# A banded attention and a softplus MLP on one core: a new start order, score bursts and a new written order

## The chip, the cores and the metric

The kernel runs on one core of a Trainium2 chip. The metric is the device time of one execution in microseconds (us), as the median of several runs. The engines are PE (TensorE, matrix products), DVE (VectorE), ACT (ScalarE), POOL (GpSimd) and SP, which here only issues DMAs. PEld is PE's loading of weights, which overlaps its products.

## The reference

Attention with four batches, eight heads, 768 rows and a head dimension of 64. A row sees eight global keys and the 96 keys up to itself; a bias grows with the distance, and the slope depends on the head. The attention's output, 3072 tokens of 512 values, goes through two products with a softplus between them.

```python
scores = scale * np.matmul(q, k.transpose(0, 1, 3, 2))
is_global = pos[None, :] < int(n_global)            # 8
is_local = (rel >= 0) & (rel < int(n_local))        # 96
dist = np.where(is_global & ~is_local, float(n_local), np.abs(rel))
scores = scores - slopes[:, None, None] * dist      # per head
a = softmax of scores where (is_global | is_local)
x = (a @ v), rows of 8 heads side by side           # 3072 x 512
h = x @ w_in                                        # 512 x 2048
g = np.maximum(h, 0.0) + np.log1p(np.exp(-np.abs(h)))
return g @ w_out                                    # 2048 x 512
```

## The kernel before

The work is cut into 24 blocks of 128 query rows with all eight heads, and into twelve units of two neighbouring blocks of a batch, 256 rows. Blocks, units and tiles are counted from zero here. Every step is a named operation with an engine, the buffers that it reads and writes, and a function that emits its instructions. One long written table, `ORDER`, lists all names with the letter of their engine (P for PE, V for DVE, A for ACT, G for POOL, S for SP). The operations are emitted in that order, so the table is each engine's queue, and an engine works its queue strictly in order; a semaphore wait is added where an operation reads or overwrites what another engine made.

The names that matter here, with the lines of the kernel before:

- `ldq`, `ldk`, `ldv`: loads of a unit, 512 KB of each (L584, L598, L608); the first units' q and k come in halves of 256 KB. `win` and `wout` are the eight tiles of each weight, 512 KB apiece (L639). SP issues them all but the first q (ACT). They land in 14 slots called `raw`, and a slot is used again when its cast has been made.
- `castq`, `castk`, `castv`, `cin`, `cout`: casts to bf16 (L658, L674, L686, L706, L643).
- `trq`, `trk`: transposes of q and k. For the first three units PE makes them into PSUM (L790 for unit 0, in two halves; L810 after) and `cpq`, `cpk` copy them out (L793, L817); later units use DMA transposes that SP issues (L837, L830).
- `sc n`: the scores of block n on PE (L950; L897 for block 0), against the block's own keys and, for all but the first block of a batch, against those of the block before, whose first rows have been replaced by the batch's global keys. `gk` and `gv` make these copies of the global rows of k (L852, L855) and v (L868). A block's scores lie in two parts (`n.0`, `n.1`), each in one of two PSUM tiles `s_ps0` and `s_ps1`.
- `z n`: the bias added by DVE (L976); for blocks 0 and 1 PE puts the bias in before the scores instead (`sb`, L887 and L931). `ex n`: the exponential on ACT (L983). `pv n`: P·V on PE (L1002). `nm n`: a reciprocal and a product on DVE that normalise (L1013, L1014).
- `xt n`, `xc n`: the transpose of a block's x, on PE for the first six blocks (L1033, L1038), then by a DMA transpose (L1045).
- `a g.p`: for the 256 tokens of unit g the products with tile p of w_in, eight on PE (L1060), into one of two PSUM tiles `h_ps`; `e` (L1075) and `ln` (L1086) are the two ACT steps of the softplus.
- `b`: the products with w_out. Groups 0 and 1 use plain ones (L1107); later groups use a scheme with seven instead of eight products of half size (L521), for which `ws` adds up parts of w_out once (L416) and `ka` parts of the activations per group (L451), on DVE or POOL; `oe` adds the results up.
- `oc`, `st`: copies and stores of the output.
- `fill`: a 128x512 product on a constant tile `blank` into `x_ps` (L1235). Nothing uses its result.

Two things about the first unit and the bursts are set by small tables. The two halves of the first transposes of q and of k go through one and the same PSUM tile, so the second half can be made when the first has been copied out. `WHOLE` names the blocks whose two score parts are one operation of sixteen products; the others make one part, wait until its tile can be written again, and make the second. In the kernel before blocks 1, 3 and 5 are not in it.

```python
WHOLE = (0, 2, 4, 6, 7, 8, 9, 10, ..., 23)
FIRST_LOADS = "k0 q0 v0 q1 k1 v1 i1 i3 i0 i2 i4 i5 i7 i6 k2 q2 o0 ...".split()
for parts in () if n in LONE else ((0, 1),) if n in WHOLE else ((0,), (1,)):
    scores(n, parts, rank + 0.1 * parts[0])
```

## Time and profile before

| what | value |
|---|---|
| median of 3 runs | 210.56 us (210.1 to 210.59) |
| span of the profiled execution | 208.3 us |
| difference, around the span | 2.26 us |
| PE busy | 201.5 us, 97% |
| ACT busy | 169.0 us, 81% |
| DVE busy | 159.8 us, 77% |
| POOL busy | 112.8 us, 54% |
| mean granted PE clock | 0.997 |

The span runs from the first to the last instruction of the profiled execution; the time of a run is a little longer. Busy shares are means over the span. Whether an engine sets the time is read from stretches of it: PE's busy time in a stretch beside the stretch's length, and what released PE after a gap. In a row of the timeline the first number is the start, the second the duration, and brackets hold the idle time before and its releaser. In rows of groups the numbers after the bar are the busy time in us and the mean of one in ns; the row of a source line has minimum, median and maximum in ns.

### The profile page before, as it was taken

What the parts mean: (1) busy time and instruction counts of PE and PEld (TensorE: products, weight loads), DVE (VectorE), ACT (ScalarE), POOL (GpSimd) and SP (SyncE); (2) the same over time, 40 slices, a digit from 0 to 9 for tenths busy, and PEclk for the clock granted to TensorE, in tenths of its full rate; (3) what the DMA queues carried; (4) which work ended last, traced back from release to release, by engine and by line L of the source; (5) the groups of instructions that cost most, each with busy time, mean ns of one, the idle gap of its engine ahead of it and who ended that gap; (6) DMA issues with size and microseconds to landing.
All of it is one profiled execution on the core that took longest, in us unless ns stands there. A gap on an engine that the chain in (4) does not pass through costs nothing.

```text
span 208.3 us, 5515 instructions
## 1 busy us (share of the span) xinstructions
PE 201.5 (97%) x2211; PEld 164.8 (79%) x2211; DVE 159.8 (77%) x296; ACT 169.0 (81%) x240; POOL 112.8 (54%) x127
## 2 busy tenths in 40 slices
PE   7789999999999999999999999999999999999993
PEld 2455887756678889888888898888888889888882
DVE  5589899899888798786989995928897684434383
ACT  4698899998999987998879989679879895897300
POOL 4356262708686367742867699655707506623540
PEclk9999999999999999999999999999999999999998
DMA  5999999999998999679999979573742204200205
GB/s 175 364 361 388 387 358 361 332 245 249 201 271 214 257 210 312 172 188 296 195 212 259 191 200 221 145 152 102 106 73 62 92 5 142 63 0 0 104 22 181
DMA packets 70650, 40.99 MB, mean 197 GB/s; under 512 B 30433, under 2 KB 62689, under 8 KB 70625
## 3 DMA queue, kind: packets, MB, share of 16 engines
q1 hardware_dynamic: 69936, 39.99, 77.2%
q10 hardware_dynamic: 688, 0.66, 1.0%
q8 instruction: 17, 0.28, 0.5%
q14 instruction: 9, 0.07, 0.1%
HBM read 27.26 MB, written 6.29 MB: 161 GB/s over the span
## 4 chain that ended last, share of the span: by engine, by line
PE 85%; DMA 8%; DVE 2%; POOL 2%; issue 1%; ACTq 0%; ACT 0%; POOLq 0%; DVEq 0%
PE h_ps L1060 38%; PE o_ps L521 25%; PE s_ps L950 5%; PE x_ps L1002 4%; PE s_ps L1107 3%; DMA raw<-in_q_dram 3%; DMA kT<-kb 3%; DMA XT<-xs 2%; PE x_ps L1235 2%; PE x_ps L521 2%; PE s_ps L521 1%; PE s_ps L810 1%; POOL vb L706 1%; PE o_ps L1107 1%; PE o_ps L1002 1%
## 5 line engine op out<-in xcount | busy, mean ns | idle before, releaser
L1060 PE MATMUL h_ps<-XT,w_in_bf 128*128 128x256 bf16 x768 | 94.4, 273 | 0.1
L1060 PEld LDWEIGHTS <-w_in_bf 128*128 128x128 bf16 x768 | 73.2, 98 | 11.0 <-DMA XT<-xs 0.3
L1075 ACT ACTIVATE e<-h_ps 128x512 f32<-128x512 f32 x96 | 60.1, 637 | 17.6 <-PE h_ps L1060 16.6
L1086 ACT ACTIVATE g<-e 128x1024 bf16<-128x1024 f32 x48 | 49.8, 1053 | 0.6
L976 DVE TENSOR_TENSOR z<-s_ps,biasA 128x1024 f32<-128x1024 f32 x38 | 45.9, 1218 | 3.5 <-PE s_ps L950 3.1
L983 ACT ACTIVATE pb<-z 128x1024 bf16<-128x1024 f32 (+1 forms) x44 | 43.4, 993 | 1.3 <-DVE z L976 0.6
L451 POOL TENSOR_TENSOR g<-g 128x1024 bf16<-128x1024 bf16 x11 | 23.9, 2171 | 23.7 <-DVE raw L451 23.5
L521 PEld LDWEIGHTS <-g 128*128 128x128 bf16 x320 | 30.9, 98 | 3.6
L451 POOL TENSOR_TENSOR raw<-g 128x1024 bf16<-128x1024 bf16 x9 | 19.6, 2177 | 15.0 <-ACT g L1086 13.5
L868 POOL COPY vb<-vb 4x512 bf16<-4x512 bf16 x22 | 14.9, 675 | 20.9 <-PE x_ps L1002 16.2
L706 POOL CAST vb<-raw 64x512 bf16<-64x512 f32 x32 | 21.6, 678 | 6.0 <-DMA raw<-in_v_dram 4.7
L521 PEld LDWEIGHTS <-raw 128*128 128x128 bf16 x240 | 22.6, 98 | 2.8
L521 PE MATMUL o_ps<-raw,raw 128*128 128x256 bf16 x192 | 24.3, 273 | 0.0
L451 DVE TENSOR_TENSOR raw<-g 128x1024 bf16<-128x1024 bf16 x21 | 17.2, 829 | 6.5 <-ACT g L1086 4.1
L521 PE MATMUL o_ps<-raw,g 128*128 128x256 bf16 x160 | 19.6, 273 | 0.0
L1002 PEld LDWEIGHTS <-pb 128*128 128x128 bf16 x352 | 16.4, 98 | 3.6 <-ACT pb L983 0.6
L1014 DVE TENSOR_TENSOR xs<-x_ps,rcp 128x256 bf16<-128x256 f32 x40 | 17.0, 424 | 1.4
L1002 PE MATMUL x_ps<-vb,pb 128*128 128x65 bf16 x304 | 15.8, 193 | 0.0
L521 PE MATMUL o_ps<-w_out_bf,g 128*128 128x256 bf16 x128 | 15.8, 273 | 0.0
L1235 PE MATMUL x_ps<-blank 128*128 128x512 bf16 x35 | 11.7, 454 | 1.2 <-DVE blank L1159 1.2
L1013 DVE RECIPROCAL rcp<-x_ps 128x4 f32<-128x4 f32 x40 | 7.1, 178 | 7.4 <-PE x_ps L1002 6.8
L674 POOL CAST qb<-raw 128x1024 bf16<-128x1024 f32 (+1 forms) x9 | 9.3, 1032 | 5.9 <-DMA raw<-in_q_dram 5.6
(123 smaller groups left out, 216.3 us busy)
## 6 DMA issues: line engine op xcount, KB each, us to landing
raw<-in_v_dram SPq DMA_DIRECT2D x12, 512.0 KB, 5.7
out_dram<-osb SPq DMA_DIRECT2D x22, 256.0 KB, 2.5
raw<-in_q_dram SPq DMA_DIRECT2D x9, 512.0 KB, 4.9
raw<-in_k_dram SPq DMA_DIRECT2D x9, 512.0 KB, 5.5
raw<-in_moe_w_in_dram SPq DMA_DIRECT2D x8, 512.0 KB, 9.3
raw<-in_moe_w_out_dram SPq DMA_DIRECT2D x8, 512.0 KB, 9.1
raw<-in_k_dram SPq DMA_DIRECT2D x6, 256.0 KB, 5.9
raw<-in_q_dram SPq DMA_DIRECT2D x4, 256.0 KB, 7.0
```

Source lines behind the costliest of these rows:

```text
L451: (nc.vector if eng == "DVE" else nc.gpsimd).tensor_tensor(dst, a[0], b[0], ALU.subtract)
L521: nc.tensor.matmul(psum(j), lhs[:, f // 2, f % 2, :], w(f), start=(f == 0 and not (chain and j in "267")), stop=(f == 7), skip_group_check ...
L706: copy_on[eng](dst, src)
L868: copy_on[eng](vb_of(prev)[sl, :, 0:D], vb_of(first)[sl, :, 0:D])
L976: nc.vector.tensor_tensor(z, src, bias, ALU.add)
L983: nc.scalar.activation(pb[:, 0:nr, :].rearrange("p (y a) b -> p y (a b)", y=2), src, AF.Exp, scale=1.0 / root_d)
L1002: nc.tensor.matmul(xv[:, h, :], pb[:, 4 * (h % 2) + 2 * part + h // 2 if lone else u_all * (2 * (h % 2) + h // 2) + u, :], vb_of(prev if u ...
L1014: nc.vector.tensor_tensor(xs[:, 4 * part : 4 * part + 4, :], xv[:, :, 0:D], rcp[:][:, :, None].to_broadcast([P, 4, D]), ALU.mult,)
L1060: last = nc.tensor.matmul(hv[:, j, :], w_in_bf[:, m, fb * P : fb * P + P], XT[g % NXG][:, m, :], start=(m == 0), stop=(m == NM - 1),)
L1075: nc.scalar.activation(e[:, p % 2, :, :].rearrange("p j (b t r) -> p (j b) r t", b=2, r=2), hb[:].rearrange("p (a r t) -> p a r t", a=4, r=2),
L1086: nc.scalar.activation(gt[:, 2 * p - 2 : 2 * p + 2, :].rearrange("p a t -> p (a t)"), e[:].rearrange("p a j t -> p (a j t)"), AF.Ln, bias=1.0,
L1235: nc.tensor.matmul(x_ps[:], blank[:, 0:P], blank[:])
```

## The change

First, the table `ORDER` is written anew up to the middle of the kernel; from there on it differs in single places. Second, the list of first loads is put in another order, and with it the queue of SP. Third, the halves of unit 0's transposes get a PSUM tile each: q's use `s_ps0` and `o_ps`, k's `s_ps1` and `x_ps`. Fourth, blocks 1, 3 and 5 join `WHOLE`. Fifth, 28 fillers instead of 35: eleven at the start of the program and 17 after unit 0's casts and transposes have been declared; ten of them stand ahead of the first transposes in PE's queue, and the rest between later operations. Sixth, the copies of global rows no longer carry a dependency on the exponentials of the block before. Seventh, the two slots for the sums of w_out are set aside when the sums are made, not when the first tile of w_out is loaded. Line numbers move by one to four.

```diff
 ORDER = """
-ident:G ldv0:S ldq0.0:A blank:V fill0:P ldk0.0:S iota:G table:A ldq0.1:A fill1:P ldk0.1:S fill2:P dl1a:V dl0a:V
+iota:G ldk1.1:S ldq0.0:A blank:V fill0:P ldk0.0:S table:A ldq0.1:A ident:G dl0a:V fill1:P dl1a:V dl0b:V fill2:P
...
-FIRST_LOADS = "k0 q0 v0 q1 k1 v1 i1 i3 i0 i2 i4 i5 i7 i6 k2 q2 o0 o1 v2 o2 o3 o4 o5 o6 o7".split()
+FIRST_LOADS = "k0 q0 v0 q1 k1 v1 i0 i1 i2 i3 k2 q2 i4 i5 o0 o1 i6 i7 o2 o3 v2 o4 o5 o6 o7".split()
...
-FILLERS = 35
+FILLERS = 11, 28
...
+SPLIT_KEYS = {"q": (("s", 0, 0), ("o",)), "k": (("s", 1, 0), ("x",))}
...
-WHOLE = (0, 2, 4, 6, 7, 8, 9, 10, 11, 12, 13, 14, 15, 16, 17, 18, 19, 20, 21, 22, 23)
+WHOLE = (0, 1, 2, 3, 4, 5, 6, 7, 8, 9, 10, 11, 12, 13, 14, 15, 16, 17, 18, 19, 20, 21, 22, 23)
...
-        if held and not spare:
-            spare.extend(idle.popleft() for _ in range(2))
...
     def weight_sums(rank):
 
         at = {p: raw_of["out", p] for p in range(NSLOT)}
+        spare.extend(idle.popleft() for _ in range(2))
...
-                tr = s_ps[key[1]][:, x, :].bitcast(BF16)[:, 0:512]
+                home = SPLIT_KEYS[which][x]
+                tr = bank(home).bitcast(BF16)[:, 0:512]
...
-    def globals_k(n, rank, since):
+    def globals_k(n, rank):
...
-           reads=kt_keys(first), writes=kt_keys(prev), after=since, port=True,
+           reads=kt_keys(first), writes=kt_keys(prev), port=True,
...
-    def filler(j):
-
+    def fillers(js):
         def fn():
             nc.tensor.matmul(x_ps[:], blank[:, 0:P], blank[:])
 
-        return op(f"fill{j}", "PE", 0.216, 1e6 + j, fn, reads=["blank"],
-                  after=[pl.writer[("x",)]] if j else [])
+        for j in js:
+            last = op(f"fill{j}", "PE", 0.216, 1e6 + j, fn, reads=["blank"], after=users(("x",)))
+            pl.writer[("x",)], pl.readers[("x",)] = last, []
...
             attend_in(i, at_block(n0) - 6.0)
+            if not i:
+                fillers(range(*FILLERS))
```

The first place is SP's queue at its start. A row is the line, the instruction, its output and input with the numbers of the buffers, and the size; "x2" means twice in a row. Before:

```order
L608 DMA raw2_69<-in_v_dram 128x8x128
L584 DMA raw0_67<-in_k_dram 128x2x256 x2
L598 DMA raw4_71<-in_k_dram 128x1x512
L598 DMA raw3_70<-in_q_dram 128x1x512 x2
L598 DMA raw4_71<-in_k_dram 128x1x512
L608 DMA raw5_72<-in_v_dram 128x8x128
L598 DMA raw1_68<-in_k_dram 128x1x512
L639 DMA raw8_75<-in_moe_w_in_dram 128x2x512
L639 DMA raw6_73<-in_moe_w_in_dram 128x2x512
L639 DMA raw7_74<-in_moe_w_in_dram 128x2x512
L639 DMA raw9_76<-in_moe_w_in_dram 128x2x512
L598 DMA raw2_69<-in_q_dram 128x1x512 x2
```

And the same place of the changed kernel:

```order
L597 DMA raw4_71<-in_k_dram 128x1x512
L583 DMA raw0_67<-in_k_dram 128x2x256 x2
L607 DMA raw2_69<-in_v_dram 128x8x128
L597 DMA raw3_70<-in_q_dram 128x1x512 x2
L597 DMA raw4_71<-in_k_dram 128x1x512
L638 DMA raw6_73<-in_moe_w_in_dram 128x2x512
L607 DMA raw5_72<-in_v_dram 128x8x128
L638 DMA raw7_74<-in_moe_w_in_dram 128x2x512
L597 DMA raw11_78<-in_q_dram 128x1x512
L597 DMA raw10_77<-in_k_dram 128x1x512
L638 DMA raw9_76<-in_moe_w_in_dram 128x2x512
L597 DMA raw11_78<-in_q_dram 128x1x512
```

The first v moves behind the first k, and a half of unit 1's k comes ahead of all; unit 2's q and k move in between the first w_in tiles. Behind these rows four (before) or five (after) further w_in tiles follow ahead of the first tile of w_out.

The second place is DVE's queue around the bias adds of blocks 4 and 5 (L976 before, L974 after); `raw3_70<-raw5_72,raw6_73` and its like are the sums of w_out (L416), `w_in_bf` the last cast of w_in on DVE. Before:

```order
L643 CAST w_in_bf_116<-raw12_79 128x2x512
L1038 COPY XT1_119<-o_ps_66 128x4x128
L976 TENSOR_TENSOR z1_95<-s_ps0_61,biasA_128 128x1024
L976 TENSOR_TENSOR z2_96<-s_ps1_62,biasA_128 128x1024
L416 TENSOR_TENSOR raw3_70<-raw5_72,raw6_73 128x512 x2
L643 CAST w_out_bf_117<-raw13_80 128x1024
L416 TENSOR_TENSOR raw3_70<-raw5_72,raw6_73 128x512
L706 CAST vb_93<-raw7_74 64x8x64
L416 TENSOR_TENSOR raw3_70<-raw5_72 128x512
L416 TENSOR_TENSOR raw4_71<-raw13_80,raw8_75 128x512
```

And after:

```order
L974 TENSOR_TENSOR z1_95<-s_ps0_61,biasA_128 128x1024
L974 TENSOR_TENSOR z2_96<-s_ps1_62,biasA_128 128x1024
L1011 RECIPROCAL rcp3_115<-o_ps_66 128x4
L1012 TENSOR_TENSOR xs0_101<-o_ps_66,rcp3_115 128x256
L642 CAST w_in_bf_116<-raw3_70 128x2x512
L974 TENSOR_TENSOR z1_95<-s_ps1_62,biasA_128 128x1024
L1036 COPY XT1_119<-o_ps_66 128x4x128
L866 COPY vb_93<-vb_93 4x8x64
L974 TENSOR_TENSOR z0_94<-s_ps0_61,biasA_128 128x1024
L415 TENSOR_TENSOR raw12_79<-raw2_69 128x512
```

Block 4's bias adds now stand ahead of the last w_in cast and both of block 5's right behind it; before, block 5's came after the first sums of w_out. On PE block 5's sixteen score products stand ahead of a0.6 and a0.7 now, and behind P·V of block 4 before.

The third place is DVE's queue from the first bias add of block 9 on; `raw..<-g..` and `g..<-g..` are token sums (L451 before, L450 after). Before:

```order
L976 TENSOR_TENSOR z2_96<-s_ps0_61,biasA_128 128x1024
L976 TENSOR_TENSOR z0_94<-s_ps1_62,biasA_128 128x1024
L1013 RECIPROCAL rcp1_113<-x_ps_63 128x4
L1014 TENSOR_TENSOR xs2_103<-x_ps_63,rcp1_113 128x256
L451 TENSOR_TENSOR raw11_78<-g2_109 128x1024
L1013 RECIPROCAL rcp2_114<-x_ps_63 128x4
L1014 TENSOR_TENSOR xs0_101<-x_ps_63,rcp2_114 128x256
L451 TENSOR_TENSOR g2_109<-g2_109 128x4x2x128
L451 TENSOR_TENSOR raw12_79<-g2_109 128x1024
L1013 RECIPROCAL rcp3_115<-x_ps_63 128x4
L1014 TENSOR_TENSOR xs0_101<-x_ps_63,rcp3_115 128x256
L976 TENSOR_TENSOR z2_96<-s_ps1_62,biasA_128 128x1024
```

And after:

```order
L974 TENSOR_TENSOR z2_96<-s_ps0_61,biasA_128 128x1024
L1011 RECIPROCAL rcp0_112<-x_ps_63 128x4
L1012 TENSOR_TENSOR xs2_103<-x_ps_63,rcp0_112 128x256
L705 CAST vb_93<-raw7_74 64x8x64
L450 TENSOR_TENSOR raw9_76<-g2_109 128x1024
L974 TENSOR_TENSOR z0_94<-s_ps1_62,biasA_128 128x1024
L450 TENSOR_TENSOR raw10_77<-g2_109 128x1024
L866 COPY vb_93<-vb_93 4x8x64
L450 TENSOR_TENSOR raw9_76<-g2_109 128x1024
L866 COPY vb_93<-vb_93 4x8x64
L1011 RECIPROCAL rcp1_113<-x_ps_63 128x4
L1012 TENSOR_TENSOR xs2_103<-x_ps_63,rcp1_113 128x256
```

The last row before is the first bias add of block 10. After, it comes later: an output copy, two token sums, two normalisations and an output add still stand ahead of it, and block 10's second bias add follows it at once. Two P·V operations of block 8 move behind block 9's scores on PE; the cast of unit 4's k (`castk4.0`) moves from POOL to ACT, behind the exponential of a2.2; and the DMA transpose of block 7's x moves ahead of that of unit 5's q.

157 lines of the change are left out of this document (76 added, 81 removed).

## The prediction

> **What bounds the kernel now.** I read the head of the page first, then the busy time by stretch.
>
> ```profile
> span 208.3 us, 5515 instructions
> PE 201.5 (97%) x2211; PEld 164.8 (79%) x2211; DVE 159.8 (77%) x296; ACT 169.0 (81%) x240; POOL 112.8 (54%) x127
> PE 85%; DMA 8%; DVE 2%; POOL 2%; issue 1%; ACTq 0%; ACT 0%; POOLq 0%; DVEq 0%
> ...
> 0.00:10.00 10.00, 7.64 (x37) 3.41 (x37) 5.74 (x21) 6.15 (x15) 4.34 (x14) 1.00 0.82 267
> ...
> 25.00:28.43 3.43, 3.43 (x50) 2.78 (x48) 3.02 (x9) 2.88 (x5) 1.65 (x2) 1.00 1.05 385
> 28.43:38.50 10.07, 10.07 (x105) 7.58 (x101) 9.38 (x16) 9.70 (x13) 5.45 (x7) 1.00 1.12 342
> ...
> 56.00:66.00 10.00, 9.80 (x122) 7.44 (x120) 8.86 (x15) 9.67 (x14) 7.03 (x12) 1.00 1.22 236
> 66.00:80.00 14.00, 14.00 (x168) 12.32 (x166) 12.59 (x22) 11.74 (x17) 8.52 (x13) 1.00 1.20 259
> ...
> 140.00:180.00 40.00, 40.00 (x469) 35.31 (x468) 29.70 (x52) 33.37 (x47) 20.09 (x14) 1.00 0.37 86
> 180.00:208.30 28.30, 24.71 (x227) 21.88 (x224) 13.36 (x23) 12.65 (x18) 9.26 (x5) 0.98 0.16 57
> ```
>
> In the rows by stretch the columns are the stretch, its length, the busy time of PE, PEld, DVE, ACT and POOL, the clock, the DMA share and GB/s. From 28.43 us on PE loses nothing but 0.20 us at 56–66 us and what the drain at the end costs. So the order can win only in the first 28 us and in that 0.20, and it can lose wherever PE now has no gap. The time after 28.43 us follows from how much of PE's fixed work is done by then.
>
> What sets 28.43 us is seen in the timeline of the start and in the DMA view of the first 28 us.
>
> ```profile
> 1.17 4.90 PE L1235 MATMUL x_ps<-blank 128*128 128x512 bf16 x12 [1.17 <-DVE blank L1159]
> 5.65 0.62 ACT L658 CAST qb<-raw 128x512 bf16<-128x512 f32 x1 [0.45 <-DMA raw<-in_q_dram]
> ...
> 7.90 0.87 DVE L658 CAST kb<-raw 128x512 bf16<-128x512 f32 x1 [0.87 <-DMA raw<-in_k_dram]
> ...
> 18.85 1.03 PE L1060 MATMUL h_ps<-XT,w_in_bf 128*128 128x256 bf16 x8
> ...
> 19.98 1.04 POOL L643 CAST w_in_bf<-raw 128x1024 bf16<-128x1024 f32 x1 [1.57 <-DMA raw<-in_moe_w_in_dram]
> ...
> 27.39 0.71 DVE L643 CAST w_in_bf<-raw 128x1024 bf16<-128x1024 f32 x1 [0.37 <-DMA raw<-in_moe_w_in_dram]
> 28.43 1.92 PE L1060 MATMUL h_ps<-XT,w_in_bf 128*128 128x256 bf16 x16
> ```
>
> ```profile
> q1 hardware_dynamic: 6493, 8.92, 91.6%
> ```
>
> The start is a stream of loads on one queue, 8.92 MB in 28 us at a 91.6% share. Ahead of the eighth w_in tile lie the q, k of three units and two v, eight tiles of 512 KB, and the eight w_in tiles: 8.4 MB. That tile is cast at 27.39 + 0.71 = 28.10, and the pair of products that needs it (a0.7, a0.6) starts at 28.43.
>
> **The change, part by part.**
>
> *Loads.* Before, v0 (512 KB) is issued ahead of the first k; now a 256 KB half of k. At the 385 GB/s of 25–28 us this brings the first q half forward by 262144 / 385000 = 0.68 us, so its cast starts near 5.0 and the last k half near 7.2. With the second halves in banks of their own no transpose waits for the copy of the first half, and block 1's exponentials should come some 2 us sooner, the first product of w_in near 16.8 instead of 18.85. This lead isn't kept. The bytes ahead of the eighth w_in tile are the same sixteen tiles, so its cast still starts near 27.4 and PE meets the same gate near 28.4. q2, k2 and the third w_in tile come no sooner, and PE waits for them at 19–24 us. The lead is worth only what PE can finish before the gate that it did after it before.
>
> *Warm-up.* 28 instead of 35 fillers, all before the gate: ten ahead of the first transposes instead of twelve, the rest in waits. They run on a bank that nothing waits for there; seven fewer cost and bring nothing, hidden by the wait for the loads. If too many stood behind a landed tile, one would cost 4.90 / 12 = 0.41 us cold, and that delay also ends at the gate.
>
> *Blocks 1, 3, 5 in one burst.* Before, the halves of block 5's scores share a bank and lie after the gate; the chain of waits has them:
>
> ```profile
> 35.38 0.33 PE s_ps L950 x8
> ...
> 38.23 0.34 PE s_ps L950 x8
> ...
> 52.39 5.58 DMA kT<-kb
> ...
> 58.02 0.62 PE s_ps L950 x16
> ...
> 60.56 4.29 DMA XT<-xs
> ...
> 64.90 1.92 PE h_ps L1060 x16
> ...
> 68.57 0.87 PE h_ps L1060 x8
> 69.44 0.24 PE x_ps L1002 x8
> ...
> 77.57 0.55 PE s_ps L950 x16
> ```
>
> Now all 16 products stand ahead of a0.6 and a0.7, in time in which PE waits for tiles. That takes 0.33 + 0.34 = **0.67 us** from the work behind the gate. Bounds: 0, if PE comes to the gate late, and 0.67 + 0.33 (28.43 − 28.10), if a0.6 starts as soon as the tile is cast. I take 0.67. Behind the gate e0.5 now stands behind block 4's last exponential on ACT, at most one product's slack of 0.27 us: I take **+0.1**.
>
> *The 0.20 us at 56–66.* The gaps are the landings of block 8's keys (57.97) and of block 7's x (64.85). Before the first PE now has a2.4 and a2.5 ahead, less one pair of w_out products, 2 × 0.87 − 0.43 = 1.3 us more to do: the gaps close, **−0.2**. But castk4.0, which feeds that key transpose, moves from POOL to ACT, behind e2.2. PE has 3 × 0.87 + 6 × 0.43 + 3 × 0.24 + 0.62, 6.1 to 6.5 us, between a2.2 and block 8's scores, against 0.64 (exponential) + 1.05 (cast) + the DMA:
>
> ```profile
> DMA to landing us min/median/max: 2.6/4.2/6.9
> 32.53 0.43 PE s_ps L1107 x2
> 51.32 1.05 POOL kb L686
> L1075 ACT ACTIVATE e<-h_ps 128x512 f32<-128x512 f32 x96 | 60.1, 637 | 17.6 <-PE h_ps L1060 16.6
> ```
>
> With the median of 4.2 that is 5.9, in time; with 5.58 it is 7.3, 1.2 late. I take 0, since the loads and transposes queued ahead are the same ones. The transpose of block 7's x has 4.0 us of PE work after it (2 × 0.87 + 4 × 0.43 + 0.55) against 0.6 + 4.29, 0.9 late; but that 4.29 was spent behind a q transpose which now is issued after it. I take 0, bounds 0 and 0.9.
>
> *Engines.* By the order DVE gets seven more casts of v, seven more of q, five more copies of v's global rows and two more token sums, and gives six weight sums to POOL. The global copies no longer wait for the exponentials of the block before; that wait costs PE nothing now, and nothing is counted for it. The tightest place is DVE from block 9's bias add to the end of block 10's.
>
> ```profile
> L976 DVE TENSOR_TENSOR z<-s_ps,biasA 128x1024 f32<-128x1024 f32 x38 | 45.9, 1218 | 3.5 <-PE s_ps L950 3.1
> L1014 DVE TENSOR_TENSOR xs<-x_ps,rcp 128x256 bf16<-128x256 f32 x40 | 17.0, 424 | 1.4
> L1013 DVE RECIPROCAL rcp<-x_ps 128x4 f32<-128x4 f32 x40 | 7.1, 178 | 7.4 <-PE x_ps L1002 6.8
> L451 DVE TENSOR_TENSOR raw<-g x21: 670/692/2044, 68.2 to 194.9; 128x1024 bf16<-128x1024 bf16 x21
> L868 DVE COPY vb<-vb 4x512 bf16<-4x512 bf16 x7 | 3.5, 496 | 0.1
> L706 DVE CAST vb<-raw 64x512 bf16<-64x512 f32 x11 | 5.4, 493 | 0.2
> L485 DVE TENSOR_TENSOR osb<-osb,o_ps 128x512 f32<-128x512 f32 x8 | 5.5, 686 | 5.0 <-ACT pb L983 1.8 <-PE o_ps L521 1.7 <-ACT e L1075 1.4
> 28.36 2.34 DVE L976 TENSOR_TENSOR z<-s_ps,biasA 128x1024 f32<-128x1024 f32 x2
> ```
>
> There now stand 4 bias adds, 4 normalisations (178 + 424), 5 token sums, 2 copies, one cast and 2 output adds: 4.87 + 2.41 + 3.46 + 0.99 + 0.49 + 1.37 = 13.6 us. Before it was 4, 3, 4, 1, 0, 1: 10.6. Block 11's scores need both banks, so they wait for the last of it. PE's work in between is 77.57 − 64.90 = 12.7, plus two P·V groups that move into the stretch, 13.2. Back to back DVE would be 0.4 late, and 1.1 with 0.7 for a sum that waits for the last logarithm of its group. Neighbouring instructions overlap, though: two bias adds took 2.34, not 2.44, so 18 instructions give back up to 1.8. Bounds 0 and 1.1; nearer to the overlap, **+0.1**.
>
> ACT at 56–66 stands at 9.67 of 10.00. The cast of 1.05 more would overfill it by 0.72; bounds 0 and 0.72, and I take 0, because at 28–38 it stood at 9.70 of 10.07 and PE lost nothing.
>
> *Sum.* −0.67 + 0.1 − 0.2 + 0.1 = −0.67. The profiled execution has a span of 208.3 us, the median of the runs is 210.56, 2.26 more for what lies around the span; so 207.6 + 2.26, **209.9 us**. About 0.3%, 0.63 us, is what a measurement can tell from no change, so this lies at its edge.
>
> **The rivals.**
>
> *More than that.* The third w_in tile's cast waited 1.57 us for its DMA at 19.98, a gap of some 1.4 us in an otherwise even stream. If the new order isn't hit by it, every later tile comes 1.4 us sooner and the gate with it: 208.5. For it: the lead of 2 us would be there to use it. Against it: nothing in the order names a cause.
>
> *ACT hands it back.* The 0.72 us of the overfilled stage stand against the 0.67: 210.6, no change. For it: 97% busy there. Against it: 28–38 us.
>
> *Slower: DVE becomes the bound between blocks 9 and 11.* If it runs back to back, 1.1 us are lost at block 11's scores, and one of the five sums held as long as the slowest of its row, 2044 − 692 ns, adds 1.35: 209.9 − 0.1 + 2.45 = 212.2. It decides once more than 1.4 us are lost there. The trace has that slow sum. The Trainium skill, page "SBUF — State Buffer", section "SBUF: two separate sides", says that VectorE and GpSimd share one port pair as an exclusive lock, and that the loser blocks for the whole instruction. That speaks against putting sums on DVE beside POOL's casts; the 2044 ns of the row agree with it, the median of 692 shows that it is rare. By the rule one such sum makes it 212.2, by the median 209.9.
>
> *Slower: the transposes land late.* 1.2 us at block 8's keys and 0.9 at block 7's x: 209.9 + 2.1 = 212.0, and it decides from 1.3. Against it: the queue order just told.
>
> **How the numbers follow.** The forecast's case, 209.2 to 210.6, has 0.44 (0.28 below 209.93, 0.16 within); the larger gain 0.10; ACT 0.18 (0.02 faster, 0.13 within, 0.03 slower); DVE 0.16 and the transposes 0.12, both slower. Together 0.40 faster, 0.29 the same, 0.31 slower. The range reaches from 208.7, which leaves out half of the larger gain (0.05), to 212.0, which leaves out about half of the two slower cases (0.13).
>
> **What would show it.** The first cast of q near 5.0 us, the first product of w_in near 16.8, and yet the last w_in cast near 27.4 with a0.6 at 28.1 to 28.5 and block 5's 16 score products ahead of it. After that PE should be as full as before: a gap on PE ahead of block 11's scores, released by DVE's bias add, would speak for DVE; one ahead of block 8's scores or of a3.1, released by a DMA, for the transposes; small ones after exponentials at 55–65 us for ACT. The prediction is wrong at its root if the last w_in tile lands a microsecond or more away from 27.4, or if PE arrives at it late.

## The result and the profile after

The changed kernel takes 216.39 us (median of 4 runs, 215.72 to 217.72) against 210.57 (210.10 to 210.94) of the kernel before: a ratio of 1.0284, 95% interval 1.0248 to 1.032. It is 5.8 us slower. A ratio in this text compares a kernel with runs of the kernel before made beside it (medians from 210.36 to 210.89) and leaves out a single run more than 1.5% above its kernel's fastest, so it can differ by some tenths of a per cent from the quotient of two medians. The profiled execution has a span of 213.8 us, 5.5 more than before.

The head of the page of the changed kernel, with the shares of the chain that ended last:

```profile
span 213.8 us, 5476 instructions
PE 202.4 (95%) x2195; PEld 164.4 (77%) x2204; DVE 162.4 (76%) x307; ACT 170.6 (80%) x243; POOL 106.0 (50%) x113
PE 70%; DMA 12%; DVE 10%; ACT 3%; SPq 2%; issue 1%; DVEq 0%; ACTq 0%
```

On the chain PE falls from 85% to 70%; DMA rises from 8 to 12, DVE from 2 to 10. The busy time by stretch, changed kernel, with the columns of the prediction:

```profile
28.43:38.50 10.07, 9.96 (x105) 8.18 (x102) 8.95 (x16) 9.27 (x14) 7.84 (x7) 1.00 1.09 355
38.50:47.00 8.50, 8.45 (x64) 5.02 (x64) 7.29 (x16) 8.25 (x11) 4.67 (x5) 1.00 0.79 210
47.00:56.00 9.00, 8.76 (x99) 6.40 (x99) 8.84 (x14) 7.38 (x11) 7.36 (x9) 1.00 1.13 273
56.00:66.00 10.00, 8.59 (x93) 5.77 (x95) 8.28 (x16) 9.95 (x14) 4.78 (x8) 1.00 1.06 177
66.00:80.00 14.00, 13.61 (x169) 11.72 (x167) 13.62 (x27) 12.84 (x18) 5.03 (x8) 1.00 1.05 221
80.00:100.00 20.00, 19.53 (x237) 16.80 (x235) 17.78 (x33) 17.64 (x24) 3.73 (x5) 1.00 1.01 225
100.00:140.00 40.00, 38.30 (x435) 32.64 (x432) 30.12 (x56) 31.72 (x45) 26.27 (x28) 0.96 1.03 210
```

In these rows PE is idle for 0.11 + 0.05 + 0.24 + 1.41 + 0.39 + 0.47 + 1.70 = 4.37 us, against 0.20 before. The row of 100 to 140 us also has a clock of 0.96. From 140 to 180 us PE is busy for 40.00 of 40.00 us, as before. PE's last product ends 5.95 us later than before, and what comes behind it is 0.46 us shorter (3.13 instead of 3.59), so the span grows by 5.5. The gate is here what the prediction calls so: the cast of the last w_in tile, for which a0.6 and a0.7 wait. The waits of PE behind the gate, changed kernel (who waits, for whom; us in total, times, the longest):

```profile
PE h_ps L1058 <- DMA XT<-xs: 2.0, 2, 1.6
PE o_ps L1105 <- ACT osb L1134: 1.0, 1, 1.0
PE x_ps L1000 <- DVE xs L1012: 0.4, 1, 0.4
PE s_ps L948 <- DMA kT<-kb: 0.4, 1, 0.4
```

Four of five are late transposes or what a late load held up; the one on DVE is small. **The start**, in the timeline of the changed kernel:

```profile
27.85 0.69 DVE L642 CAST w_in_bf<-raw 128x1024 bf16<-128x1024 f32 x1
28.06 0.63 PE L948 MATMUL s_ps<-qT,kT 64*128 64x128 bf16 x16
28.86 1.96 PE L1058 MATMUL h_ps<-XT,w_in_bf 128*128 128x256 bf16 x16
```

The work begins sooner (the cast of a q half at 4.67 us, the first w_in product at 17.50), but the last w_in tile is cast at 27.85 + 0.69 = 28.54 instead of 28.10, and block 5's products stand in front of the gate while it opens. a0.6 starts 0.43 us later than its counterpart before, with 0.67 us of products already done: a net lead of 0.24 us.

**Where the first wait comes from.** SP's queue around unit 3's v, before and then after (start, duration, place, instruction):

```profile
37.78 0.42 SPq L608 DMA_DIRECT2D raw<-in_v_dram  x1
39.49 1.04 ACT L674 CAST qb<-raw 128x1024 bf16<-128x1024 f32 x1
40.56 2.70 SPq L837 DMA_TRANSPOSE qT<-qb  x1
43.43 0.45 SPq L608 DMA_DIRECT2D raw<-in_q_dram  x1
43.98 1.54 SPq L830 DMA_TRANSPOSE kT<-kb  x1
45.62 0.55 SPq L608 DMA_DIRECT2D raw<-in_k_dram  x1
46.22 1.26 SPq L830 DMA_TRANSPOSE kT<-kb  x1
```

```profile
41.60 0.67 DVE L673 CAST qb<-raw 128x1024 bf16<-128x1024 f32 x1
42.31 1.34 SPq L835 DMA_TRANSPOSE qT<-qb  x1
43.76 0.51 SPq L607 DMA_DIRECT2D raw<-in_v_dram  x1
44.41 1.21 SPq L828 DMA_TRANSPOSE kT<-kb  x1
45.67 0.57 SPq L607 DMA_DIRECT2D raw<-in_q_dram  x1
46.30 1.67 SPq L828 DMA_TRANSPOSE kT<-kb  x1
48.17 0.42 SPq L607 DMA_DIRECT2D raw<-in_k_dram  x1
```

Before, the load of v3 is issued ahead of the transpose of q3. After, it stands behind that transpose, and the transpose waits for a cast that now is made on DVE and 2.1 us later. SP works in order, so v3 is issued 6.0 us later. But the issue of q3's transpose is over at 43.65 us, only 0.4 us later than before, since it takes 1.34 instead of 2.70 us. What makes the next loads late is what now stands ahead of them: v3 and the first of k3's two transposes ahead of q4, which is issued 2.2 us later, and the second one ahead of k4. Before, that second one came behind k4. So k4 is issued 2.55 us later, and then takes 6.53 us to land instead of 5.04. The same nine microseconds by stretch, before and then after:

```profile
39.00:48.00 9.00, 9.00 (x71) 5.46 (x69) 8.91 (x16) 8.51 (x13) 2.04 (x4) 1.00 1.14 278
```

```profile
39.00:48.00 9.00, 8.95 (x68) 5.37 (x68) 7.79 (x16) 8.73 (x13) 5.45 (x5) 1.00 0.82 210
```

The stream of loads is (278 − 210) GB/s × 9 us = 0.6 MB behind at 48 us. What follows is in the chain of waits of the changed kernel:

```profile
48.17 6.53 DMA raw<-in_k_dram
54.80 1.05 ACT kb L685
55.85 0.53 ACT e L1073
56.37 0.47 ACT osb L1134
56.88 0.38 PE o_ps L1105
...
107.28 3.85 DMA XT<-xs
111.13 0.05 issue
111.18 1.82 PE h_ps L1058 x8
```

k4 lands at 54.70. Its cast, on ACT now, holds ACT's queue until then, the exponential and the output copy behind it come late, and PE waits 1.05 us. Before, the same cast ran on POOL at 51.32.

**The last wait** is the second half of the chain. At 86 us v7, too, stands behind transposes (SP's queue and DVE, changed kernel):

```profile
86.21 0.67 DVE L673 CAST qb<-raw 128x1024 bf16<-128x1024 f32 x1
86.92 1.81 SPq L835 DMA_TRANSPOSE qT<-qb  x1
88.78 2.57 SPq L1043 DMA_TRANSPOSE XT<-xs  x2
91.44 0.53 SPq L607 DMA_DIRECT2D raw<-in_v_dram  x1
```

v7 is issued at 91.44 (before at 84.38), k8 lands at 104.22 (before 98.72), and block 13's x, which comes through the queue behind k8's transpose, lands at 111.13 (before 106.67). a6.0 waits 1.59 us for it, and then runs at half the clock: its eight products take 1.82 us instead of 0.87. By the clock's own records in the trace the halved clock lasts 3.41 us, and PE is busy for all of it (the stretch before it and this one):

```profile
107.88:111.29 3.41, 1.71 (x25) 1.16 (x20) 3.38 (x7) 1.28 (x2) 2.07 (x2) 1.00 0.73 116
111.29:114.70 3.41, 3.41 (x23) 2.57 (x22) 2.29 (x5) 1.25 (x2) 1.53 (x3) 0.50 0.99 259
```

Put together for the profiled execution: 4.37 us idle, less the 0.20 of before, less the lead of 0.24, plus 1.7 for 3.41 us at half the clock, make 5.6 of the 5.95 us by which PE's last product ends later.

### The profile page after: what moved, and what is told of

It is laid out like the page before. It is cut to its first block, busy times and chain, and to the rows that moved or that the text cites. A ratio compares the mean times of both kernels' runs of the same rounds, so it can differ in the third digit from the quotient of the medians.

```text
span 213.8 us, 5476 instructions
## 1 busy us (share of the span) xinstructions
PE 202.4 (95%) x2195; PEld 164.4 (77%) x2204; DVE 162.4 (76%) x307; ACT 170.6 (80%) x243; POOL 106.0 (50%) x113
## 4 chain that ended last, share of the span: by engine, by line
PE 70%; DMA 12%; DVE 10%; ACT 3%; SPq 2%; issue 1%; DVEq 0%; ACTq 0%
PE h_ps L1058 32%; PE o_ps L520 21%; PE s_ps L948 4%; PE x_ps L1000 4%; DMA raw<-in_k_dram 3%; DMA raw<-in_q_dram 3%; PE s_ps L1105 3%; DVE z L974 3%; DMA kT<-kb 2%; DMA XT<-xs 2%; PE x_ps L520 2%; PE o_ps L1105 1%; DVE raw L450 1%; DMA out_dram<-osb 1%; PE s_ps L520 1%
## 5 line engine op out<-in xcount | busy, mean ns | idle before, releaser
L1058 PE MATMUL h_ps<-XT,w_in_bf 128*128 128x256 bf16 x768 | 96.9, 275 | 2.1 <-DMA XT<-xs 2.0
L1084 ACT ACTIVATE g<-e 128x1024 bf16<-128x1024 f32 x48 | 49.3, 1049 | 0.5
L974 DVE TENSOR_TENSOR z<-s_ps,biasA 128x1024 f32<-128x1024 f32 x38 | 45.8, 1216 | 3.4 <-PE s_ps L948 3.2
L450 POOL TENSOR_TENSOR g<-g 128x1024 bf16<-128x1024 bf16 x11 | 23.8, 2169 | 34.2 <-DVE raw L450 32.7
L450 POOL TENSOR_TENSOR raw<-g 128x1024 bf16<-128x1024 bf16 x7 | 15.4, 2194 | 15.4 <-ACT g L1084 13.7
L450 DVE TENSOR_TENSOR raw<-g 128x1024 bf16<-128x1024 bf16 x23 | 17.7, 777 | 6.0 <-ACT g L1084 3.5
L705 POOL CAST vb<-raw 64x512 bf16<-64x512 f32 x23 | 15.6, 678 | 10.6 <-DMA raw<-in_v_dram 9.7
L673 POOL CAST qb<-raw 128x1024 bf16<-128x1024 f32 (+1 forms) x6 | 6.6, 1101 | 13.5 <-DMA raw<-in_q_dram 9.1
L685 POOL CAST kb<-raw 128x1024 bf16<-128x1024 f32 x6 | 7.0, 1169 | 11.1 <-DMA raw<-in_k_dram 11.0
L866 POOL COPY vb<-vb 4x512 bf16<-4x512 bf16 x16 | 9.9, 616 | 2.6 <-PE x_ps L1000 1.4
```

What stands on the lines that cost most here:

```text
L450: (nc.vector if eng == "DVE" else nc.gpsimd).tensor_tensor(dst, a[0], b[0], ALU.subtract)
L705: copy_on[eng](dst, src)
L866: copy_on[eng](vb_of(prev)[sl, :, 0:D], vb_of(first)[sl, :, 0:D])
L974: nc.vector.tensor_tensor(z, src, bias, ALU.add)
L1058: last = nc.tensor.matmul(hv[:, j, :], w_in_bf[:, m, fb * P : fb * P + P], XT[g % NXG][:, m, :], start=(m == 0), stop=(m == NM - 1),)
L1084: nc.scalar.activation(gt[:, 2 * p - 2 : 2 * p + 2, :].rearrange("p a t -> p (a t)"), e[:].rearrange("p a j t -> p (a j t)"), AF.Ln, bias=1.0,
```

## The experiments

The theory after the result: the change loses by the order of SP's one queue and by the casts that feed its transposes; the start costs nothing, and DVE is not the bound. The rivals: the start loses, DVE is the bound, or the halved clock is the cost.

### One part of the change alone, from the side of the kernel before

**The start.** The changed kernel up to z5.0, the order of before behind it. The first form had a bad seam, as the place is called here where the two orders meet: b0.0.0 writes an `s_ps` tile and so waited 0.99 us for block 5's bias add, and e0.7 stood behind two logarithms for 0.85 us.

```diff
 ... xc3:V e0.6:A gv4.0:V z5.0:V
-(the changed order)
+gk8:G gv8.1:G ln0.1:A ln0.2:A e0.7:A ldq3:S ... (the order of before)
```

> The start of the changed kernel up to block 5's bias adds, with all parts of the change in it, and behind it the order and the engines of the kernel before for all that is left. Theory that the losses all lie behind 30 us (queue, DVE, clock): as fast as before or better by what the start gained, 209.9 to 210.8. Theory that the start already does the harm (warm-up, first loads, bursts): 212 or more.

213.28 us, ratio 1.0133 (1.0104 to 1.0162). The two seam waits come to 1.84 us, but they are read in the fastest of its five runs (211.69), which lies 0.8 us above the kernel before. So this settled nothing. The second form has e0.7 ahead of the logarithms.

> As the mix of the changed kernel's start and the old rest, with the seam mended: the first products of w_out (b0.0.0, b0.0.2) stand behind a1.1 and a1.0, since they share PSUM tiles with block 5's scores and waited 0.99 us for its bias add, and e0.7 stands ahead of two logarithms that it waited 0.85 us for. Theory that the start itself is neutral or good: both waits go, 1.5 to 2 us better than the mix before, 211.0 to 211.8 by its median. Theory that the start does harm of its own (bursts block the tiles of the first w_out products): no better than 212.5.

211.30 us, 1.0023 (1.0004 to 1.0041), with seam waits of 0.72 and 0.46 us left. The third form swaps a1.0 and a1.1, puts e0.5 ahead of block 4's last exponential, has SP's queue as before from the first w_out tile on, and moves a cast and two global copies.

```diff
-sc5.0:P ex4.1:A wout4:S xt3:P z5.1:V a0.6:P e0.5:A ... a1.1:P b0.0.0:P ... a1.0:P
+sc5.0:P e0.5:A ex4.1:A wout4:S xt3:P z5.1:V a0.6:P ... a1.0:P e1.0:A ln0.2:A b0.0.0:P ... a1.1:P
```

> The start of the changed kernel with the old rest, with the seam mended further: a1.0 ahead of a1.1 and their exponentials likewise, e0.5 ahead of block 4's last exponential, SP's queue from the first tile of w_out on exactly as before, one cast of v earlier on DVE. The mix before it (211.3) had waits of 0.72, 0.46 and 0.23 us at the seam. Theory that the start is worth the 0.67 us of block 5's scores: 209.7 to 210.2. Theory that the start is worth nothing, since PE reaches the last w_in tile late: 210.5 to 211.

210.71 us, 1.0018 (0.9993 to 1.0042). The profiled execution, with a span of 207.8 us, is 0.5 us shorter than that of before, but it is the fastest of ten runs that spread from 209.82 to 212.10; those of before lie between 210.11 and 211.19. With SP's queue of before behind it, the new start with block 5's burst is worth nothing that can be measured, and it doesn't cost the 5.8 us either.

**DVE.** The kernel before with the extra work that the change gives DVE at blocks 8 to 10.

```diff
-castv4.11:G gv9.1:G gv9.0:G ka2.6:G
+castv4.11:V gv9.1:V gv9.0:V ka2.6:V   (behind z9.0, nm8.1, nm8.1 and ka2.7)
```

> The kernel before with the four operations that the run with less on DVE gave back put on DVE here: castv4.11 behind block 9's first bias add, gv9.1 and gv9.0 behind the normalisation nm8.1, ka2.6 behind ka2.7; 2.2 us more for DVE between 65 and 78 us. DVE theory (there DVE was busy 12.6 of 14 us, so 2.2 us more make it the bound): 211.4 to 213, PE waiting for nm9.0, nm9.1 or block 10's bias add. Theory that DVE has the room, since POOL's slower versions were waited for as well: 210.4, within 0.5.

The busy time by stretch of this kernel:

```profile
66.00:80.00 14.00, 14.00 (x166) 12.25 (x165) 13.69 (x25) 11.80 (x17) 5.96 (x9) 1.00 1.19 246
```

210.70 us, 1.0006 (0.9991 to 1.0021). DVE is busy for 13.69 of 14.00 us, more than in the changed kernel (13.62), and PE loses nothing. The converse in the changed kernel:

```diff
-castv4.11:V gv9.1:V gv9.0:V ka2.6:V
+castv4.11:G gv9.1:G gv9.0:G ka2.6:G
```

> The changed kernel with four operations given back from DVE to POOL at their places in the table: a cast of unit 4's v (castv4.11), the two copies of the global rows of v for block 9 (gv9.0, gv9.1) and one token sum (ka2.6), together 2.2 us of DVE work ahead of block 9's and 10's normalisations. DVE theory: the two waits of P.V of block 9 for DVE (some 0.8 us with the lag of 1.4 us that is built up between 64 and 80 us) go, 214.9 to 215.7; if the later waits are inherited from there, 212 or less. Queue theory: at most 1 us better, the wait of 1.59 us at unit 6's first products and the slow clock stay, 215.4 to 216.4.

216.49 us, 1.0283 (1.0232 to 1.0333): no gain. Giving the work back makes a wait of its own, though (PE waits 0.86 us at 75.92 for POOL's copy of v's global rows), so the first of the two is the better test: the work that the change adds on DVE at blocks 8 to 10 doesn't bound PE. For DVE's other places no run tests it.

**The order of SP's queue.** The kernel before with three loads of v behind the transposes where the change puts them; nothing else moves.

```diff
 SP's queue
-ldv3 trq3 ldq4
+trq3 ldv3 ldq4
-ldv6 trk5.1 xt9 ldq7 trq6 st1.0.0
+trk5.1 xt9 ldq7 trq6 ldv6 st1.0.0
-ldv7 trk7.0 xt11 st2.0.0
+trk7.0 xt11 ldv7 st2.0.0
```

> The kernel before with the same three loads delayed on SP's queue, nothing else: v of unit 3 behind trq3, v of unit 6 behind trq6, v of unit 7 behind the transpose of block 11's x. Queue theory: 212 to 215, with waits of PE for transposes or casts between 50 and 115 us. If the loads have slack there: 210.6, within 0.4.

The longest wait of PE in this kernel; the first casts on POOL behind v6; and its stretch of 80 to 100 us beside the one of before (last):

```profile
PE x_ps L1002 <- POOL vb L868: 1.8, 1, 1.8
```

```profile
81.41 1.63 POOL L706 CAST vb<-raw 64x512 bf16<-64x512 f32 x2 [6.38 <-DMA raw<-in_v_dram]
```

```profile
80.00:100.00 20.00, 17.68 (x213) 15.22 (x211) 14.20 (x24) 16.32 (x22) 12.65 (x14) 1.00 0.85 202
```

```profile
80.00:100.00 20.00, 20.00 (x238) 17.35 (x237) 15.29 (x28) 18.63 (x26) 11.37 (x13) 1.00 0.99 226
```

213.99 us, 1.016 (1.0137 to 1.0182): three moved issues cost the kernel before 3.4 us. v6 is issued at 76.44 (69.61 before), and POOL, which also works in order, stands still for 6.38 us until it has landed. PE waits at 85 us for a cast of v5 that comes behind v6's on POOL (84.67 us), and at 87 us for POOL's copy of v's global rows behind that; these two waits make up the 2.32 us that PE lacks there. A third, of 1.15 us at 109.6, is for an output add on DVE. The loads flow at 202 instead of 226 GB/s. The granted clock was 1.00 in all four runs, so this cost is waiting alone. The first of the three moves hardly delays k4, which lands at 50.78 here, at 50.66 before.

**The casts ahead of the transposes.** The kernel before with q3, q4 and k4 cast on the engines of the change.

```diff
-castq3.0:A castq4.0:A castk4.0:G
+castq3.0:V castq4.0:V castk4.0:A   (behind ws1.1, z6.1 and e2.1)
```

> The kernel before with three casts moved as the change moves them, SP's order untouched: castq3.0 from ACT to DVE (ready near 42.3 us instead of 40.5), castq4.0 from ACT to DVE (53.0 instead of 49.4), castk4.0 from POOL to ACT behind the exponential of a2.1 (55.6 instead of 52.4). Queue theory (a cast that comes late holds SP's queue at its transpose, and all loads behind it): the load stream falls 1 to 3 us behind at 53 us and PE waits for block 8's keys and for x's transposes, 212 to 214.5. Theory that only the loads' places matter and casts have slack: 210.4, within 0.5.

Its longest wait, and that wait's link in the chain:

```profile
PE s_ps L950 <- DMA kT<-kb: 1.6, 1, 1.6
```

```profile
55.20 0.92 ACT kb L686
56.14 4.41 DMA kT<-kb
```

213.22 us, 1.0123 (1.0077 to 1.0169), 2.6 us. k4 is cast at 55.20 instead of 51.32, its transpose lands at 60.55, and block 8's scores wait 1.60 us. The load of k4 is hardly late here: it lands at 51.11 (50.66 before). Its cast stands in ACT's queue behind exponentials that wait for DVE's bias adds, and DVE, with the casts of q3 and q4 added, is busy for 8.97 of 9.00 us at 39–48 us and for 8.80 of 9.00 at 48–57 (8.91 and 8.34 before). So DVE does matter in another way than as PE's bound: how full its queue is sets when a cast is made and when the transpose behind it can go. Two runs with a mean clock of 1.00 took 212.34 and 212.49, two with 0.99 took 213.96 and 214.17: by these four, waiting costs 1.8 us, and a lower clock, where it comes, another 1.6.

So the two causes, each put into the kernel before by itself, cost 3.4 and 2.6 us, 6.0 together, beside the 5.8 of the whole change. The two weren't run together, so that they add is not shown. Nor does the near agreement show each one's share: in these two kernels PE waits for POOL at 85 and 87 us, for an output add at 109.6 and for block 8's keys at 60, in the changed kernel at other places and for other things. Shown is that each is by itself large enough to lose microseconds in a kernel that had lost 0.20. The other moves between engines were not tried one by one.

### The changed order up to a point, that of before behind it

The changed kernel's table is kept up to sc6.0, sc9.0 or sc11.0, about 50, 65 and 80 us.

```diff
 ... ldk4:S gv8.0:A ldv4:S sc6.0:P
-(the changed order)
+(the order of before)
```

> The changed kernel's order and engines up to block 6's scores (49 us), the old order behind. Theory that each stage loses on its own: PE was level with before at 48 us, so 210.5 to 211.5, and the 5.8 us lie in the order behind. Theory that the loss is inherited from the load stream, which falls 0.6 MB behind at 39 to 48 us: 213 us or more, with waits of PE for transposes at 56 to 65 and 95 to 115 us.

> The changed order up to block 9's scores (64 us), the old order behind. Stage by stage: PE was 0.8 us behind there, so 211.3 to 212.3; the overloaded DVE queue of blocks 9 to 11 isn't in it. Inheritance: 214 us or more. If DVE between 64 and 80 us is the cause of the rest, this one is free of it and the next one has it: a step of 3 us or more between the two.

> The changed order up to block 11's scores (79 us), the old order behind, where PE's order is the same in both and only the queues of SP, DVE, ACT and POOL differ. Stage by stage: PE was 1.4 us behind there, so 212 to 212.8, and the last 4 us come from the queues behind 79 us, SP's first of all (v of unit 7 stands behind trq7, which waits for a cast on DVE). Inheritance: 215.5 to 216.5, as the whole change.

They took 213.13 (1.0089), 213.12 (1.0107) and 215.73 (1.0239). The first has one wait at its seam, 2.41 us for an exponential at 54.6, the third one of 2.32 us at 89.7 for a global copy of v on POOL. Less these waits the first shows about 0.1 us and the third 2.8, which speaks for a loss that comes after 50 us. It is no proof: the waits are read in one run of each, two of the first kernel's four runs and the profiled one of the third had a mean clock of 0.992, and that the third's wait comes from the seam and not from a late load isn't shown. More than this the series can't say. In the second the wait of 1.05 us at 57 stands as in the changed kernel, and there are two more of 0.75 and 0.30.

### Mending the changed kernel

**v3 ahead of trq3** in SP's queue:

```diff
-ws1.7:V trq3:S cout6:A ... nm5.0:V b1.0.4:P ldv3:S
+ws1.7:V ldv3:S trq3:S cout6:A ... nm5.0:V b1.0.4:P
```

> The changed kernel with one load moved on SP's queue: unit 3's v ahead of the transpose of unit 3's q (trq3), as in the kernel before. Nothing else moves. Queue theory (a load behind a transpose that waits for its cast leaves the DMA engines idle, and PE pays later): the dip of the load stream at 42 to 45 us goes, unit 4's k lands 1 to 2 us sooner than 54.7, ACT is not held by castk4.0 and the wait of 1.05 us at the w_out products behind it shrinks; 0.5 to 2 us better, 214.4 to 215.9. Theory that the late loads have slack everywhere: 216.4, within 0.5.

215.56 us, 1.0246 (1.0193 to 1.0299). The wait at 56 us shrinks from 1.05 to 0.32, by about as much as k4 lands sooner (53.95 instead of 54.70), but 0.84 at 65, 1.50 at 80 and 1.83 at 112 us stand in its place. So by this execution v3's place is 0.75 of the 4.0 us by which k4 is late. With v3 out of the way SP waits 0.5 us for POOL's cast of k3 and 0.5 for a weight sum on POOL, and issues k4 at 47.99 us, 0.2 sooner than without the mend.

**v6 and v7 forward**, alone and with v3:

```diff
 SP's queue
-xt8 xt9 ... trq6 ldv6 ... st2.0.0 trq7 xt10 xt11 ldv7
+xt8 ldv6 xt9 ... trq6 ... ldv7 st2.0.0 trq7 xt10 xt11
```

> The changed kernel with two loads moved on SP's queue: unit 6's v from behind trq6 to behind the transpose of block 8's x, unit 7's v from behind the transposes of blocks 10's and 11's x to ahead of trq7. Queue theory: the dips at 75 to 81 and 90 to 93 us go, unit 8's k and block 13's x come 2 us sooner or more, the wait of 1.59 us and the half clock behind it go; 213 to 214.5. If the transposes of x wait for their normalisations on DVE instead: no better than 215.9.

> The changed kernel with all three loads moved. Queue theory: the two gains add up, 212.5 to 213.8, and what is left to the kernel before is DVE at 64 to 80 us and the seam of the start. No queue effect: 216.4, within 0.5.

217.83 (1.0342, 1.0297 to 1.0387) and 217.57 (1.0319, 1.0266 to 1.0372): not better. a6.0's wait falls from 1.59 to 0.33 us in the first, though block 13's x lands no sooner (114.44 instead of 111.13): PE itself comes later, since block 9's x now is issued right behind v6, lands at 83.34 behind that load (82.70), and a4.0 waits 2.83 us. Not all of that is the edit's: in the kernel with v3 forward, without this edit, a4.0 waits 1.50. But there blocks 8 and 9 have their x landed within 0.5 us of one another, and here block 9's comes 2.41 us after block 8's. In this place a load ahead of a transpose held up its landing; behind it, the load's own issue had been held up.

**Block 13's x forward**, right behind block 12's; **castk4.0 on POOL**; and both with v3 forward:

```diff
-nm13.1:V b4.3:P ... gk15:G a5.7:P xt13:S
+nm13.1:V xt13:S st2.1.0:S b4.3:P ... gk15:G a5.7:P
```

> The changed kernel with one transpose moved on SP's queue: that of block 13's x (xt13) right behind that of block 12's x, ahead of the store st2.1.0, the transpose trk8.0 (which waits for a cast of unit 8's k until 105.3 us) and the store st3.0.0. Its input is ready at 103.8 and it is issued at 107.3 now. Theory that this one late landing makes the last and largest loss: it lands near 108 instead of 111.1, the wait of 1.59 us at a6.0 and the half clock behind it (some 1.7 us) go, 213.1 to 213.6. Theory that PE is held there by something else that is as late (unit 8's keys, DVE's normalisations): 215.5 or above.

```diff
-castk4.0:A
+castk4.0:G
```

> The changed kernel with the cast of unit 4's k (castk4.0) on POOL, as before, instead of ACT. Theory that ACT is stuck behind the late load of k (54.7 us) and holds the copy that the w_out products at 56.9 us wait for: that wait of 1.05 us goes, 215.2 to 215.8 if the gain is kept, 216.4 if the later waits take it. Theory that POOL, stuck in ACT's place, delays its weight sums instead: no gain or slower, 216.4 to 217.

> The changed kernel with three single mends: xt13 moved forward as alone, castk4.0 on POOL, unit 3's v ahead of trq3. If the losses are separate: the gains add up, 3.0 + 0.6 + 0.8, 211.8 to 212.8. If one pool of lateness is only handed on: no better than the best of them alone.

216.57 (1.027), 216.92 (1.0295) and 214.36 (1.0175, 1.0135 to 1.0214). Each of the first two removes the wait at which it aims, and neither moves the time beyond its spread. Other waits stand in the profiles: 1.28 us at 67.4 and 1.50 at 82.7 in the first, 0.71 for POOL's global copy and 2.08 at 113 in the second. That the mend makes them isn't shown. Those of the first lie ahead of its edit, which begins near 104 us, in a stretch where it runs the same order as the changed kernel, and that one waited 0.40 at 65 and not at all at 82. So the waits differ by a microsecond and more from one execution to the next, and a mend of that size can't be told in four runs. The three together save 2 us, less than was expected, and are the only mend that is clear of the noise.

**SP's queue in before's order**, from ldq3 on, with the rest of the changed kernel as it is:

```diff
 SP's queue
-ldq3 wout6 ldk3 wout7 trq3 ldv3 trk3.0 ldq4 trk3.1 ldk4 ldv4 ldq5 trq4 ...
+ldq3 ldk3 wout7 wout6 ldv3 trq3 ldq4 trk3.0 ldk4 trk3.1 ldv4 trq4 ldq5 ...
```

> The changed kernel, with nothing altered but SP's queue: from the load of unit 3's q on it has the order of the kernel before, so that the loads of units 3, 4, 7 stand ahead of the transposes (trq3, trq4, trq7) that wait for casts. Queue theory (SP's waits for those transposes starve the load stream, and PE pays at 56, 65, 97 and 111 us): the last wait of 1.59 us and the slow clock behind it go, and most of the 5.8 us with them; 211.5 to 213.5. DVE theory (DVE is overloaded at 64 to 80 us and the rest is inherited from there): no more than 0.5 us better, 215.9 or above. Casts theory (the transposes are late because castq3, castq4, castq7 moved to DVE, and the loads matter little): 215 to 216.4.

225.77 us, 1.073 (1.0685 to 1.0776), the worst of all. PE waits 1.74, 1.65, 4.70 and 2.91 us at 56, 69, 92 and 107.5. The longest is for a normalisation on DVE, which stands behind DVE's cast of k7, and DVE waited 6.47 us for the load of k7. SP itself stood for 3.8 us ahead of k4, by its waits for a weight sum on DVE, so k4 was issued at 49.83, later than in the changed kernel. The order of before on SP fits the order of before on the casting engines, and with the changed one it loses more than SP's changed order does.

**The clock.** Eight products on the constant tile into `h_ps` ahead of a6.0, which add work and whose results nothing uses.

```diff
+            op("warm", "PE", 1.73, rank, warm, reads=["blank"], writes=[hkey], count=8)
```

> The changed kernel with eight products on the constant tile put on PE in front of a6.0, written to the bank that a6.0 overwrites, so that PE is busy while it waits for block 13's x. The wait itself stays. Clock theory (the half clock granted from 111.2 to 114.6 us is a consequence of 1.59 us without work and costs some 1.7 us): no slice below full clock, 1.4 to 1.9 us faster, 214.5 to 215.0. If the slow clock has another cause or its loss is caught up anyway: no change within 0.4 us, or up to 0.3 us slower.

215.33 us, 1.0237 (1.02 to 1.0273): the mean clock is 1.00 in three runs and 0.998 in one, and the median is 1 us lower, though the intervals overlap with that of the change. The clock isn't needed for the loss: in two of the changed kernel's four runs it was 0.999 and 1.00 on average, and these took 216.51 and 216.27.

No version beat both kernels.

## Why the prediction was wrong

The forecast of 209.9 us, range 208.7 to 212.0, missed 216.39 by 6.5 us, on the wrong side.

- **The step that failed** is the term for castk4.0, put at 0: "I take 0, since the loads and transposes queued ahead are the same ones." They are not the same ones. From unit 3's v on SP's order was v3, trq3, q4, trk3.0, k4, trk3.1; it is now trq3, v3, trk3.0, q4, trk3.1, k4. A transpose of k3 that came behind k4 stands ahead of it, and v3 no longer goes out while SP waits for q3's cast, but behind it. So k4 was issued 2.55 us later and landed at 54.70 instead of 50.66. No one move accounts for it: with v3 forward k4 still landed at 53.95, and in the kernel before v3 behind trq3 or a later cast of q3 left it at 50.78 and 51.11. trk3.1's place was not tried by itself, and why the load then took 1.5 us longer to land is not shown. The step's bound of 1.2 us reckoned with a late transpose of k4 and not with k4 itself landing late; ACT stood still for it, and PE waited 1.05 us at 56.88 for the output copy behind the cast. For block 7's x the reason for 0 was another one, that its 4.29 us were spent behind a q transpose which now comes later; PE waited 0.40 there, within the bound of 0.9.
- **What was not priced at all** is the later part of SP's order: v6 and v7 behind transposes. In the kernel before the three moved loads cost 3.4 us. In the changed kernel v7 is issued 7.1 us later and k8 lands 5.5 us later, and block 13's x with them; the wait for it, 1.59 us, and the halved clock behind it, 1.7, are more than half of the loss in the profiled execution. Which of the moves makes that x late stays open: with v6 and v7 forward it landed no sooner. The prediction counted the seven casts each of q and v that go to DVE as DVE's busy time only; three of the moved casts of q and k cost 2.6 us in the kernel before, as releasers of transposes.
- **The rival "the transposes land late"** was right in kind. It had a chance of 0.12 and a price of 2.1 us, at two places near 60 us. The loss went on to 115 us, and its price was 5.8. What the prediction held against it, the queue order, was the failed step.
- **Loads at the start:** the lead isn't kept, as told. The q cast at 4.67 (5.0 predicted) and the first w_in product at 17.50 (16.8) are near; the last w_in cast came at 27.85 instead of 27.4.
- **Block 5's burst, −0.67:** mis-sized. PE came to the gate late, the lower bound that was named: 0.24 us net in the trace, nothing measurable in the start alone.
- **The 0.20 us at 56–66, −0.2:** it didn't close; that stretch lost 1.41 us.
- **Warm-up, 0:** nothing in the runs speaks against it.
- **DVE, +0.1:** near enough. The waits on DVE are 0.4 us in the trace and the same work in the kernel before costs nothing. The slow sum of 2044 ns on which that rival stood did not come up between blocks 9 and 11, where one sum of the changed kernel took 1035 ns; it came later, 2055 ns at 182.41, beside a sum on POOL:

```profile
181.79 2.12 POOL L450 TENSOR_TENSOR g<-g 128x1024 bf16<-128x1024 bf16 x1
182.41 2.06 DVE L450 TENSOR_TENSOR raw<-g 128x1024 bf16<-128x1024 bf16 x1
```

The Trainium skill, page "SBUF — State Buffer", section "SBUF: two separate sides", has VectorE and GpSimd block one another for whole instructions on the port pair they share. The trace agrees: this sum ends about 0.55 us behind POOL's instruction, and the other two sums of this kernel that took over a microsecond, at 68.21 and 139.22, 0.54 us behind the POOL instruction that was under way when they began. No gap on PE follows from the sum at 182.41, and the kernel before with the extra work on DVE has no gap on PE beside its sum of 932 ns at 81.83.
- **ACT at 56–66, 0:** it was busy for 9.95 of 10.00 us, and PE waited 1.05 for it. The overfill was not the reason; ACT had stood idle ahead of that, waiting for k4.

## What to carry to other kernels

Where one in-order queue issues both loads and DMA transposes, a transpose whose source isn't ready stops every load behind it, so list what stands ahead of a load in the new order, one by one, and read a moved cast or load by the time at which the head of that queue can go, not by the bytes ahead of it. Where PE has no gap and single executions differ by a microsecond in their waits, a mend at one wait can't be judged by the wait that it removes; here three single mends left the time within the spread, and the three together saved 2 us. The order of the queue and the order of the casts belong together, so changing one back by itself can be worse than either (1.073).

## What the runs showed of the hardware

The clock. By its own records in the traces, the granted clock of PE fell to half in the middle of a run for 3.41 us at a time, and each fall came a whole number of stretches of 3.41 us after the clock had first been granted in full: 31 stretches in the changed kernel, 16 in the kernel with the moved casts. Cut into these stretches, the one ahead of the fall had PE busy for 1.71 us in the changed kernel, and for 1.60 of 3.41 us in the other (this row; in the stretch behind it, 61.08 to 64.49 us, the clock was 0.50):

```profile
57.67:61.08 3.41, 1.60 (x28) 0.84 (x25) 1.21 (x4) 3.25 (x4) 2.06 (x3) 1.00 1.03 272
```

A longer pause of 1.83 us, in the kernel with v3 forward, lay across two of the stretches, left 2.35 and 2.54 us of work in them, and no fall followed:

```profile
108.02:111.44 3.42, 2.35 (x35) 1.49 (x32) 2.95 (x7) 1.76 (x3) 2.02 (x5) 1.00 0.98 131
111.44:114.85 3.41, 2.54 (x29) 2.31 (x30) 3.02 (x6) 1.41 (x3) 1.82 (x2) 1.00 0.78 192
```

So in these traces it counts how busy PE is within one stretch, and where a pause falls in it, not the pause's length alone. Each of the falls in the middle of the eight executions that have one followed a stretch with 1.71 us of work or less, but no sharp bound is shown: two stretches of the kernel with SP's queue in before's order, with 1.52 and 1.66 us, were followed by none, and some of PE's records can be missing from a trace. A fall costs 1.7 us when PE is busy throughout, half of 3.41. The Trainium skill, page "TensorE: Matmul & The Clock Gate", section "Part 1: The HAM clock gate (the "warmup" mystery)", gives a window of about 3.4 us that runs freely, and half the clock after an idle window. The traces agree on the length and on the free running; they differ in that a window with half its time idle was enough.
